# Seven small products for eight in one block product of a sequence DFT, with its sums in accumulating DMAs

## The chip, the core and the metric

The kernel runs on one core of a Trainium2 chip. The metric is the device time of one launch in microseconds, the lower the better; the time of before is the median of three runs. A profile is one execution recorded by the hardware; its times are counted from the first instruction.

Five engines work side by side, each through its own instructions in order: TensorE (PE; PEld is its weight load), VectorE (DVE), ScalarE (ACT), GpSimd (POOL) and SyncE (SP). SP and POOL issue most DMAs, and sixteen DMA engines move the data. On-chip memory has 128 partitions; a tile named 128x1024 has 1024 numbers of four bytes in each. TensorE writes its sums into PSUM, from where ScalarE or VectorE copies them.

## The reference, cut to what matters

```python
def _A_ref(x, dft_seq_re, dft_seq_im, dft_hid_re, dft_hid_im):
    a = jnp.einsum("bsd,ed->bse", x, dft_hid_re)
    b = jnp.einsum("bsd,ed->bse", x, dft_hid_im)
    y = jnp.einsum("ts,bse->bte", dft_seq_re, a) - jnp.einsum("ts,bse->bte", dft_seq_im, b)
    return y
...
xn = _layernorm(x, axis=-1)
s = _A_ref(xn, A_dft_seq_re, A_dft_seq_im, A_dft_hid_re, A_dft_hid_im)
g = _silu(_B_ref(xn, B_w1, B_b1, B_w2, B_b2))
return x + s * g
```

x is 2048 x 512, all in float32. `_B_ref` is a layer norm and an MLP with 1792 hidden units. The change is in the last step: the real part of the DFT along the sequence, a product of a 2048 x 4096 matrix (real and imaginary DFT matrix side by side) with the 4096 x 512 stack of a and b.

## The kernel before

Every product of float32 matrices is made of three matmuls: each factor is split into a rounded part (`hi`, copied by ScalarE into the type float32r) and the rest (`lo`, a subtraction on VectorE), and hi·hi, hi·lo and lo·hi are added in PSUM (`split_into`, L61). A split of a 128x1024 tile is thus one ScalarE and one VectorE instruction, the second waiting for the first, and makes two tiles.

The stages run one after the other: the layer norm and the DFT along the hidden dimension (the results a, b, and sums of their blocks, go to the DRAM tensors `a_d`, `b_d` and `s_d`), the MLP's first layer, its second (`m_units`, seven products of 7 steps each, in the order 1, 4, 2, 5, 6, 3, 7), and the DFT along the sequence.

The DFT along the sequence is a 2 x 2 block product done with seven block products for eight (Strassen-Winograd). The blocks of the left factor are a1, b1, b2 and sums s1 to s4, ready in DRAM; those of the right factor are quarters of the DFT matrices, `ct[m, h, n]` (m: real or imaginary, h: half of the sequence, n: one of 16 rows of 128), and sums of those. Each block product has 16 steps, and a step is 12 matmuls of 128x512 (`multiply_by`, L1009): two halves k of the output's rows, two halves tau of the 1024 columns, three terms. A block product's result fills two PSUM tiles of two banks each; there are four such tiles.

`passes` (L1080) pairs the products: (s4, s3), (a1, s2), (b1, b2), then s1, and b1 again for four steps that `DEFER` (L1081) leaves out of the third pass. A unit (q, n) is step n of pass q. For each unit there are three things to do ahead of its matmuls: `unit_load` (L1099) loads the left blocks (every second unit) and the right one, `unit_sum` (L1116) makes the right sums on VectorE in the held tile `t_hold[n]`, and `unit_split` (L1135) makes the splits. `ahead` (L1152) runs them a fixed number of units before the matmuls, and the loop at L1310 goes through the units; so the order of the instructions on each engine is written out by hand. The same steps for the first units are called in the MLP's last product (L1197 and after, `p == 7`).

Right sums: t = c12 - c22 (for s3), then t - c11 (s2), then c21 + t (b2, in c21's tile), and for s1 c22 is added to t: for even n by an accumulating DMA that POOL issues (L1129, the data in memory are added to the tile), for odd n by a load and a VectorE addition.

Tiles come from pools with a fixed number of places; a new tile waits until the last reader of the place is done. `op` has 39 places of 128x1024 (operands of splits, and `guest` tiles, L51), `lp` seven of the same size in the last stage (`room`, L57), `gp` four (copies of finished products).

The finished blocks are copied out of PSUM by ScalarE (`evacuate`, L1018), joined by VectorE (`after`, L1283), multiplied by the gate silu(z) (`gated`, L1267, which also adds x by an accumulating DMA), and stored (`put_out`, L1271). The last four steps of s1 and the deferred ones of b1 run piece by piece (`piece`, L1332), one quarter of the output after the other, so that the product with the gate, the sum and the store of one quarter (`end`, L1339) lie beside the matmuls of the next.

Of the kernel before, what the change touches and what calls it, by code (L numbers as in the profile page):

```python
# [14 lines left out]
P = 128  # L15
# [5 lines left out]
def fnet_mixer_kernel(ctx: ExitStack, tc: tile.TileContext, x, xT, ct, wt, w1, w2, b1, b2, out):  # L21
# [1058 lines left out]
    passes = [("s4", "s3"), ("a1", "s2"), ("b1", "b2"), ("s1",), ("b1",)]  # L1080
    DEFER = (8, 9, 10, 11)  # L1081
    units = [(q, n) for q in range(4) for n in range(NS)] + [(4, n) for n in DEFER]
    c_raw, c_left, c_ops, t_hold = {}, {}, {}, {}

    def names(q, n):
        return ("b2",) if q == 2 and n in DEFER else passes[q]


    def in_order(q, n):
        return names(q, n)[::-1 if (q, n) in ((1, 0), (2, NS - 1)) else 1]  # L1090

    at = {"load": 0, "sum": 0, "split": 0}

    def c_in(key, src, where):
        t = (guest if where == "op" else room)(f"{key}")
        nc.sync.dma_start(out=t, in_=src)
        return t

    def unit_load(u):  # L1099
        q, n = units[u]  # L1100
        if n % 2 == 0:
            t = room(f"la{q}_{n}")
            for v, name in enumerate(names(q, n)):
                nc.sync.dma_start(out=t[:, v, :].rearrange("p (c e) -> p c e", c=2), in_=left(name, n // 2))
            c_left[q, n // 2] = t
        if q == 0:
            c_raw[u] = {"s4": c_in(f"c22_{n}", ct[1, 1, n], "lp")}
            t_hold[n] = c_in(f"c12_{n}", ct[0, 1, n], "op")
        elif q == 1:
            c_raw[u] = {"a1": c_in(f"c11_{n}", ct[0, 0, n], "lp")}  # L1110
        elif q in (2, 4):
            c_raw[u] = {"b1": c_in(f"c21_{q}_{n}", ct[1, 0, n], "lp" if q == 2 else "op")}
        elif n % 2:
            c_raw[u] = {"s1": c_in(f"d22_{n}", ct[1, 1, n], "lp")}

    def unit_sum(u):  # L1116
        q, n = units[u]
        t = t_hold[n]
        if q < 2:
            raw, = c_raw[u].values()  # L1120
            nc.vector.tensor_sub(t, t, raw)  # L1121
            c_raw[u]["s2" if q else "s3"] = t
        elif q == 2:
            raw = c_raw[u].pop("b1")
            c_ops[u] = {"b1": split_two(raw, f"R2_{n}_b1")} if len(names(q, n)) == 2 else {}
            nc.vector.tensor_add(raw, raw, t)  # L1126
            c_raw[u]["b2"] = raw
            if n % 2 == 0:
                nc.gpsimd.dma_start(out=t, in_=ct[1, 1, n], accum_op=ALU.add)  # L1129
        elif q == 3:  # L1130
            if n % 2:
                nc.vector.tensor_add(t, t, c_raw[u]["s1"])  # L1132
            c_raw[u] = {"s1": t}

    def unit_split(u):  # L1135
        q, n = units[u]
        if n % 2 == 0:
            t = c_left[q, n // 2]
            who = names(q, n)
            if len(who) == 2:  # L1140
                hi, lo = split_two(t, f"L{q}_{n}")
                c_left[q, n // 2] = {name: (hi[:, v, :], lo[:, v, :]) for v, name in enumerate(who)}
            else:
                c_left[q, n // 2] = {who[0]: split(t[:, 0, :], f"L{q}_{n}")}
        ops = c_ops.setdefault(u, {})
        raw = c_raw.pop(u)
        for name in names(q, n):
            if name in raw:
                ops[name] = split_two(raw[name], f"R{q}_{n}_{name}")


    def ahead(what, until):  # L1152
        while at[what] < min(len(units), until):
# [95 lines left out]
    def kept(name):  # L1249
        return gp.tile([P, 2, W], F32, tag="g", name=name)  # L1250
# [150 lines left out]
```

## Time and profile before

| | |
|---|---|
| median of 3 runs | 665.1 us (665.03 to 665.2) |
| the profiled execution | 665.77 us, its span 664.0 us |
| matmuls in the program | 2914, PE busy 658.8 us |
| VectorE, ScalarE, POOL busy | 543.0, 361.5, 50.7 us |
| DMA | 172.81 MB, mean 260 GB/s |
| the sequence DFT's matmuls | 355.34 to 660.23 us |

How to read the rows below: a row of the chain of waits is a start, a length, an engine and a group of instructions that followed each other without a gap. A row of stretches is a time window, each engine's busy time in it with the number of its instructions, the clock granted to TensorE as a share of full speed, the mean busy share of the sixteen DMA engines, and what they moved. The DMA share adds the times that the packets took, so it can pass 1 when packets of several queues overlap. A row of a group is a line of the kernel, an engine and an operation, the tiles written and read, their shapes and a count, then busy time and mean ns of one, and the engine's idle time just before them with what ended it. A row of a tile or line has shortest, median and longest duration in ns and the first and last start.

### The profile page before, as it was taken

The page shows a single profiled execution, that of the slowest core. Times are in us where ns is not written, and L with a number is a line of the kernel's source. Part 1 is how long each engine was busy: PE and PEld are TensorE (multiplying, and loading weights), DVE is VectorE, ACT ScalarE, POOL GpSimd, SP SyncE. Part 2 cuts the span into 40 slices and gives each one's busy share as a digit, 9 for nine tenths or more (in the row PEclk, how much of TensorE's full clock was granted, in tenths as well). Part 3 has the DMA queues.
Part 4 walks back from the last instruction along what each step waited for, and adds up shares of the span by engine and source line. Part 5 has one row for each costly group of instructions (what it writes and reads, how often), then busy time and mean ns, then how long its engine had stood idle before and what let it go on. Part 6 is the DMA issues. An engine that isn't in the chain of part 4 may idle for free.

```text
span 664.0 us, 8219 instructions
## 1 busy us (share of the span) xinstructions
PE 658.8 (99%) x2914; PEld 542.8 (82%) x2914; DVE 543.0 (82%) x584; ACT 361.5 (54%) x420; POOL 50.7 (8%) x84
## 2 busy tenths in 40 slices
PE   9999999999999999999999999999999999999997
PEld 6788888888888888888888888888888888888886
DVE  7899977877777866888979998739877299998986
ACT  6775567545446755555455544456444455646540
POOL 0002000321121100000000000000000001210100
PEclk9999999999999999999999999999999999999999
DMA  9879440987989999798799996416544548996983
GB/s 321 281 254 284 147 155 1 344 313 263 350 297 358 415 412 366 267 392 306 257 396 409 365 330 223 150 57 198 184 154 130 126 134 254 308 257 242 314 255 137
DMA packets 71877, 172.81 MB, mean 260 GB/s; under 512 B 6896, under 2 KB 22812, under 8 KB 71836
## 3 DMA queue, kind: packets, MB, share of 16 engines
q1 hardware_dynamic: 59488, 132.27, 56.7%
q0 software_dynamic: 12032, 39.86, 18.9%
q8 instruction: 23, 0.38, 0.2%
q10 hardware_dynamic: 316, 0.16, 0.1%
q14 instruction: 18, 0.15, 0.1%
HBM read 121.91 MB, written 50.35 MB: 259 GB/s over the span
## 4 chain that ended last, share of the span: by engine, by line
PE 97%; ACT 1%; DVE 1%; DMA 0%; issue 0%; ACTq 0%; DVEq 0%
PE pz L1015 20%; PE px L1015 18%; PE ma L1015 11%; PE hy L830 11%; PE mb L1015 9%; PE hz L830 6%; PE pw L1015 5%; PE q1y L654 3%; PE hx L830 3%; PE pd L418 2%; PE px L1336 2%; PE pw L1336 2%; PE q1z L654 2%; PE pd L406 1%; PE quy L654 1%; PE q1x L654 1%
## 5 line engine op out<-in xcount | busy, mean ns | idle before, releaser
L1121 DVE TENSOR_TENSOR c<-c,c 128x1024 f32<-128x1024 f32 x32 | 38.9, 1216 | 4.1 <-DMA c<-ct 4.1
L81 DVE TENSOR_TENSOR w1l<-w1r,w1h 128x1792 fp32r<-128x1792 f32 x7 | 14.2, 2024 | 20.9 <-ACT w1h L525 20.9
L835 ACT ACTIVATE hc<-hc,b_t 128x1024 f32<-128x1024 f32 (+1 forms) x18 | 17.3, 960 | 24.8 <-DVE hc L875 22.6
L63 DVE TENSOR_TENSOR R_b1l<-c,R_b1h 128x1024 fp32r<-128x1024 f32 x16 | 19.4, 1220 | 13.6 <-ACT R_b1h L62 10.3
L62 ACT ACTIVATE R_s3h<-c 128x1024 fp32r<-128x1024 f32 x16 | 17.0, 1061 | 24.8 <-DVE c L1121 10.8
L1015 PE MATMUL pw<-R_s1h,L 128*128 128x512 f32 x96 | 29.7, 389 | 0.0
L62 ACT ACTIVATE R_b2h<-c 128x1024 fp32r<-128x1024 f32 x16 | 16.9, 1058 | 21.5 <-DVE c L1126 17.0
L63 DVE TENSOR_TENSOR R_s2l<-c,R_s2h 128x1024 fp32r<-128x1024 f32 x16 | 19.5, 1220 | 8.6 <-PE pz L1015 8.6
L62 ACT ACTIVATE R_s2h<-c 128x1024 fp32r<-128x1024 f32 x16 | 17.0, 1061 | 16.8 <-PE px L1015 9.3
L62 ACT ACTIVATE R_s1h<-c 128x1024 fp32r<-128x1024 f32 x16 | 16.4, 1051 | 11.7 <-DVE c L1132 11.7
L63 DVE TENSOR_TENSOR R_s3l<-c,R_s3h 128x1024 fp32r<-128x1024 f32 x16 | 19.5, 1216 | 4.0 <-PE pz L1015 4.0
L62 ACT ACTIVATE R_b1h<-c 128x1024 fp32r<-128x1024 f32 x16 | 16.7, 1053 | 10.7 <-DMA c<-ct 4.7
L1129 POOL DMA_DIRECT2D c<-ct x8 | 7.0, 872 | 201.1 <-DVE c L1126 162.9
L62 ACT ACTIVATE R_a1h<-c 128x1024 fp32r<-128x1024 f32 x16 | 16.9, 1053 | 8.9 <-PE pz L1015 7.2
L1015 PEld LDWEIGHTS pw<-R_s1h,L 128*128 128x128 f32 x96 | 18.0, 188 | 3.8
L63 DVE TENSOR_TENSOR R_b2l<-c,R_b2h 128x1024 fp32r<-128x1024 f32 x16 | 19.4, 1218 | 1.5 <-PE px L1015 1.5
L63 DVE TENSOR_TENSOR R_a1l<-c,R_a1h 128x1024 fp32r<-128x1024 f32 x16 | 19.5, 1218 | 1.3 <-PE px L1015 1.1
L63 DVE TENSOR_TENSOR R_s4l<-c,R_s4h 128x1024 fp32r<-128x1024 f32 x16 | 19.4, 1215 | 0.7 <-PE px L1015 0.7
L1126 DVE TENSOR_TENSOR c<-c,c 128x1024 f32<-128x1024 f32 x16 | 19.6, 1223 | 0.4
L62 ACT ACTIVATE R_s4h<-c 128x1024 fp32r<-128x1024 f32 x16 | 16.8, 1051 | 5.2 <-PE pz L1015 5.0
L62 ACT ACTIVATE w2h<-w 128x1024 fp32r<-128x1024 f32 (+1 forms) x14 | 13.3, 947 | 10.9 <-DVE w L943 3.9
L63 DVE TENSOR_TENSOR R_s1l<-c,R_s1h 128x1024 fp32r<-128x1024 f32 x16 | 18.8, 1218 | 0.1
(1003 smaller groups left out, 2227.3 us busy)
## 6 DMA issues: line engine op xcount, KB each, us to landing
c<-ct SPq DMA_DIRECT2D x68, 512.0 KB, 6.0
m<-h_d SPq DMA_DIRECT2D x48, 512.0 KB, 6.7
h_d<-ht POOLq DMA_DIRECT2D x21, 512.0 KB, 6.4
s_d<-sa SPq DMA_DIRECT2D x32, 256.0 KB, 4.0
la<-s_d SPq DMA_DIRECT2D x32, 256.0 KB, 6.1
h_d<-hc POOLq DMA_DIRECT2D x13, 512.0 KB, 3.9
x<-x SPq DMA_DIRECT2D x16, 256.0 KB, 5.6
sa<-a_d SPq DMA_DIRECT2D x8, 512.0 KB, 6.1
```

The source lines that it names most:

```text
L62: nc.scalar.activation(hi, src, AF.Copy)
L63: nc.vector.tensor_sub(lo, src, hi.bitcast(F32))
L81: nc.vector.tensor_sub(hi_lo[1], src, hi_lo[0].bitcast(F32))
L418: nc.tensor.matmul(dacc[i, m], xt[i, k][px], weights[m * NK + k][pw], start=seen[i, m] == 0, stop=seen[i, m] == 3 * NK - 1)
L654: nc.tensor.matmul(qx[key], a, w, start=p in (1, 5, 2) and n == 0, stop=p in (2, 3, 4) and n == len(terms) - 1, skip_group_check=True)
L830: nc.tensor.matmul(acc[:, tau, :], w[:, W1_AT[p], k * P:(k + 1) * P], r[:, k, :], start=p in (1, 5, 2) and i == 0, stop=p in (2, 3, 4) and ...
L835: nc.scalar.activation(dst, src, AF.Gelu_apprx_tanh, bias=b1_t[:, row:row + 1])
L1015: nc.tensor.matmul(acc[k][:, tau, :], a, c[:, tau, :], start=first and i == 0, stop=last and i == len(terms) - 1, skip_group_check=True)
L1121: nc.vector.tensor_sub(t, t, raw)
L1126: nc.vector.tensor_add(raw, raw, t)
L1129: nc.gpsimd.dma_start(out=t, in_=ct[1, 1, n], accum_op=ALU.add)
L1336: nc.tensor.matmul(acc[KEY[name]][k][:, tau, cols], a[k], c[:, tau, cols], start=False, stop=last and u == us[-1] and i == 2, skip_group_c ...
```

## The change

Seven block products remain, in another order and with other times for the steps ahead of them; one of them, b1, is itself done by seven small products for eight.

1. The order is a1 together with b1's small products, then (s4, s3), then (s2, s1), then b2 alone, whose last four steps go piece by piece at the end. `piece` and `end` now serve b2 alone.
2. b1: its left block (256 rows of output, from `b_d`) and its right one (`ct[1, 0]`) are cut into 2 x 2 parts. Each small product p, in the order 1, 2, 5, 3, 6, 7, 4, has four chunks of six matmuls of 128x512. The right quarters of products 1, 2, 3, 7 are loaded (runs of 2 KB); the sums for 5, 6 and 4 are made in the tiles of product 1 (`H`), each by an accumulating DMA issued after the split of the one before, and the sum for 7 by an accumulating DMA after its load. The left parts lie in one tile `wide` (pool `gp`, now one place of four times the size), loaded in 16 pieces during product 3 of the MLP, and their sums are made there by VectorE.
3. Each of the first three steps of a1 stands alone, then two chunks follow each step, and the last four chunks follow step 15.
4. s1's right sum is no longer finished for even and odd n in two ways: ScalarE copies t (after - c11) into a tile of its own, and an accumulating DMA adds c22. b2's sum is an accumulating DMA of c21 into t, issued after the split for s2.
5. In place of `ahead`, each step ahead has a due place, counted in matmuls before the product that needs it: left loads 96, splits 56, and loads and sums as in the calls below. A list sorted by due place is run as the matmuls are issued; the sort orders the instructions and doesn't hold them to these places.

```diff
-    passes = [("s4", "s3"), ("a1", "s2"), ("b1", "b2"), ("s1",), ("b1",)]
-    DEFER = (8, 9, 10, 11)
+    LEFT, SPLIT = 96, 56
...
+    def unit(names, n, load, total, load_at, total_at=0, after={}):
+        at = place[0]
+        if n % 2 == 0:
+            due(at - LEFT, then(left_in, names, n // 2))
+            due(at - SPLIT, then(left_split, names, n // 2))
+        due(at - load_at, then(load, n))
+        if total:
+            due(at - total_at, then(total, n))
+        for name in names:
+            due(at - SPLIT, then(raw_split, name, n))
+        for name in names:
+            item(12, then(multiply, name, n), [after[name]] if name in after else ())
...
+    def small_load(p, g):
+        if p == 1:
+            small_h[g] = guest(f"H{g}")
+            nc.sync.dma_start(out=small_h[g], in_=quarter(0, 0, g))
+        if p in (2, 3, 7):
+            raw_in((p, g), quarter(*{2: (1, 0), 3: (1, 1), 7: (0, 1)}[p], g), guest if p == 7 else room)
+
+    def small_sum_right(p, g):
+        nc.gpsimd.dma_start(out=raws[p, g], in_=quarter(1, 1, g), accum_op=ALU.add)
+
+    def small_split(p, g):
+        src = raws.pop((p, g)) if p in (2, 3, 7) else small_h[g]
+        small_ops[p, g] = split_two(src, f"S{p}_{g}")
+        if p in (1, 5, 6):
+            nc.gpsimd.dma_start(out=src, in_=quarter(*{1: (0, 1), 5: (1, 1), 6: (1, 0)}[p], g), accum_op=ALU.add)
...
+    def chunk(p, g):
+        at = place[0]
+        due(at - (132 if p == 7 else 108), then(small_load, p, g))
+        if p == 7:
+            due(at - 108, then(small_sum_right, p, g))
+        if g == 0:
+            if p in (5, 3):
+                due(at - SPLIT - 36, then(small_sum, p))
+            due(at - SPLIT - 6, then(small_left_split, p))
+        due(at - SPLIT, then(small_split, p, g))
+        item(6, then(small_mm, p, g), [then(small_after, p)] if g == 3 else ())
+        if g == 3 and p in (2, 6, 7):
+            due(place[0] + (0 if p == 7 else 12), then(small_add, 3 if p == 6 else p))
...
+    a_load = lambda n: raw_in(("a1", n), ct[0, 0, n], guest if n < 4 else room)
...
+    for n in range(NS):
+        unit(("a1",), n, a_load, None, 108, after={"a1": keep_1} if n == NS - 1 else {})
+        ready = 28 if n == NS - 1 else 2 * max(n - 2, 0)
+        for p, g in chunks[given:ready]:
+            chunk(p, g)
+        given = ready
...
+        unit(("s4", "s3"), n, second_load, second_sum, 132, 84,
...
+    def third_sum(n):
+        t = hold[n]
+        nc.vector.tensor_sub(t, t, raws.pop(("c11", n)))
+        raws["s2", n] = t
+        raws["s1", n] = room(f"t{n}")
+        nc.scalar.activation(raws["s1", n], t, AF.Copy)
+        nc.gpsimd.dma_start(out=raws["s1", n], in_=ct[1, 1, n], accum_op=ALU.add)
+
+    def third_late(n):
+        nc.gpsimd.dma_start(out=hold[n], in_=ct[1, 0, n], accum_op=ALU.add)
+        raws["b2", n] = hold[n]
...
+        unit(("s2", "s1"), n, third_load, third_sum, 150, 116,
...
+        due(place[0] - 24 - SPLIT, then(third_late, n))
...
-            gp = early.enter_context(tc.tile_pool(name="gp", bufs=4, reuse_waits="tile"))
+            gp = early.enter_context(tc.tile_pool(name="gp", bufs=1, reuse_waits="tile"))
...
+        if (p, j) == (3, 3):
+            small_left_in()
+        if p == 7 and j > 1:
+            run_tasks(12 * (j - NJ))
```

The joins and the gates keep their form and get new places: o (the finished b1) is joined with a1, gated and stored in the (s4, s3) stage; s4 and s3 are joined with a1 in the (s2, s1) stage; the other joins follow in the b2 stage, where s4, s3 and s1 are gated. All four blocks of two tiles add x by accumulating DMAs; three are stored by POOL, and the fourth, with b2, is finished piece by piece.

322 lines of the change are left out of this document (172 added, 150 removed).

## The prediction

> **What bounds the kernel now.** I read the page's head and its chain of waits first, then the chain in order of time, then stretches of the last stage one by one.
>
> ```profile
> span 664.0 us, 8219 instructions
> PE 658.8 (99%) x2914; PEld 542.8 (82%) x2914; DVE 543.0 (82%) x584; ACT 361.5 (54%) x420; POOL 50.7 (8%) x84
> PE 97%; ACT 1%; DVE 1%; DMA 0%; issue 0%; ACTq 0%; DVEq 0%
> ```
>
> ```profile
> 336.30 19.04 PE ma L1015 x84
> 355.34 2.72 PE px L1015 x12
> ...
> 649.10 11.13 PE px L1336 x66
> ```
>
> The chain (start, length, what, count) is TensorE back to back: 12 matmuls of 128x512 take 2.72 us, so one takes 0.2267 us. The sequence DFT begins at 355.34 and its last matmul ends at 660.23. It is bound by TensorE; fewer matmuls pay, as long as nothing else comes late. How near the others are:
>
> ```profile
> core 0: us, PE busy (x) PEld busy (x) DVE busy (x) ACT busy (x) POOL busy (x), PEclk, DMA share, GB/s
> 341.70:355.30 13.60, 13.60 (x62) 11.26 (x61) 9.80 (x9) 4.18 (x5) 0.00 (x0) 1.00 1.02 403
> 442.40:529.40 87.00, 87.00 (x385) 72.03 (x385) 65.19 (x56) 45.89 (x45) 1.77 (x2) 1.00 0.53 157
> 529.40:605.50 76.10, 76.10 (x338) 63.00 (x337) 70.20 (x63) 41.89 (x44) 10.01 (x10) 1.00 0.85 238
> 341.70:660.20 318.50, 318.50 (x1423) 264.27 (x1421) 265.90 (x249) 161.10 (x166) 17.51 (x20) 1.00 0.71 228
> 509.50:512.50 3.00, 3.00 (x15) 2.46 (x15) 2.62 (x3) 1.07 (x1) 0.00 (x0) 1.00 0.97 172
> 573.40:597.40 24.00, 24.00 (x107) 19.87 (x107) 23.58 (x21) 14.88 (x16) 6.60 (x6) 1.00 1.08 271
> ```
>
> The last two columns decide. DMA share is the packets' time over sixteen engines; 1.08, held for 24 us, is the most this trace shows, and I take it as the ceiling for mixed traffic. Plain loads fill the engines at 403 GB/s (first row), but one accumulating DMA almost alone fills them at 172 (fifth row): 0.524 MB / 172 x 0.97 = 2.96 us of all sixteen engines, where a plain 512 KB load takes 0.524 / 403 x 1.02 = 1.33. The sixth row says the same: 6 accumulates (3.15 MB) in 6.50 MB; the plain 3.36 MB cost 8.5 of 25.9 us, so 2.9 each remain. Divided by the ceilings, an accumulate takes **2.69 us** of the wall and a plain 512 KB **1.30**.
>
> **The change part by part.**
>
> *Matmuls.* Block product b1 was 16 x 12 = 192 matmuls; seven small products of 4 chunks x 6 make 168 of the same 128x512 kind. The other six products keep 192 each: 1344 become 1320. 24 x 0.2267 = **-5.4 us**, all on the chain. The end is the same code (four late pieces, then product, sum and store of quarter tiles), so what lies behind the last matmul stays; I count 0, at most 1 us either way.
>
> *VectorE and ScalarE.*
>
> ```profile
> L1121 DVE TENSOR_TENSOR c<-c,c 128x1024 f32<-128x1024 f32 x29 | 35.3, 1216 | 0.0
> L63 DVE TENSOR_TENSOR R_a1l<-c,R_a1h 128x1024 fp32r<-128x1024 f32 x16 | 19.5, 1218 | 1.3 <-PE px L1015 1.1 <-PE pz L1015 0.2
> L62 ACT ACTIVATE R_a1h<-c 128x1024 fp32r<-128x1024 f32 x16 | 16.9, 1053 | 8.9 <-PE pz L1015 7.2 <-PE px L1015 1.7
> L63 DVE TENSOR_TENSOR L<-la,L 128x512 fp32r<-128x512 f32 x12 | 8.2, 684 | 0.9 <-ACT L L62 0.9
> ```
>
> Right-hand splits go from 112 to 96 + 28 = 124 (+12), right-hand sums on DVE from 56 to 32 (-24, the accumulating DMAs take them over), left splits from 22 wide and 12 narrow to 23 and 16, small sums +4, joins of finished blocks 10 to 12, gate products 6 to 8, and 16 half-tile steps at the end go. 12 x 1.22 - 24 x 1.22 + 1.2 + 2.7 + 4.9 + 2.4 + 2.4 - 10.9 + 2 = about -10 us of DVE, and ScalarE gains 12 x 1.05 + 3.5 + 16 copies x 1.05 = 33 us on 161 in 318. Neither total is a bound. But in the first stretch (a1 with the small products) DVE is dense: until the last right split of small product 7 it has 15 + 24 splits, 8 narrow and 6 wide left splits, 4 sums, 4 joins of the MLP and some 3 splits left of it: 74 us of work, planned over 322 matmuls = 73 us, with 10 more before PE needs it. The sixth row above shows DVE at 23.58 of 24 us with PE never waiting, so alone this costs 0 to 3 us; I take 0, covered by the 56 matmuls (12.7 us) of lead. Small products share PSUM banks; each boundary has 12 matmuls of a1 (2.72 us) over a 128x512 copy or add (0.68 by the last row above): 0, at most 1 us for each of five. Stage boundaries keep the old pattern, two PSUM copies behind 12 matmuls of another product: 0.
>
> *POOL and SP.*
>
> ```profile
> L1129 POOL DMA_DIRECT2D c<-ct x8: 851/870/900, 507.8 to 587.2; - x8
> DMA to landing us min/median/max: 5.4/7.4/10.2
> L1269 POOL DMA_DIRECT2D p<-xT x6: 1195/1204/1307, 573.4 to 626.9; - x6
> DMA to landing us min/median/max: 9.5/10.6/12.5
> ```
>
> Accumulates go from 8 + 6 to 16 small + 32 + 8 gated = 56. Their issue (0.87 to 1.2 us each, some 57 us over 313) is hidden. POOL issues in order: a late DMA of the third stage (c21 into the held tile) waits for a DVE split, and the next s1 sum waits behind it. What waits for the landings is worse: ScalarE's rounding of that operand, behind it on ScalarE and VectorE every later split, and then PE. SP gets 16 strided loads of 2 KB runs in place of 4 KB ones and 16 small pieces for `wide`; both land long before use: 0. The 39 `op` tiles are tight near the end of the third stage (16 held, 12 of splits, 4 of lefts, 2 of s4, 6 of gates make 40), so a gate load may stand on SP until a product frees a tile, and b2's left loads behind it; they have 96 matmuls of lead: 0, at most 3 us.
>
> ```profile
> c<-ct SPq DMA_DIRECT2D x68, 512.0 KB, 6.0
> c<-ct POOLq DMA_DIRECT2D x8, 512.0 KB, 7.4
> p<-xT POOLq DMA_DIRECT2D x6, 512.0 KB, 10.6
> d<-ct SPq DMA_DIRECT2D x8, 512.0 KB, 6.8
> px<-xT SPq DMA_DIRECT2D x2, 512.0 KB, 6.5
> ```
>
> *The DMA engines.* Accumulates +42 x 2.9 = +122 us of packet time; plain transfers change by about nothing (80 loads for the 68 + 8 + 2 of these rows, 48 left halves for 56, `wide` added). Before, the stage holds 0.71 x 318.5 = 226 us; after, 348, and 313 us x 1.08 hold 338. So the average alone is at the ceiling, and the lulls (the row 442.40:529.40 at 0.53) don't return. If the packets of before are inflated by their own crowding, by up to a tenth, it is 325: still 96%. So two stretches in which accumulates lie close decide. I count from the first a1 matmul (place 0) in matmuls of 0.2267 us.
>
> First stretch. Small product 7's last right operand, used at place 318, must land by 298 (a split, 1.05 + 1.22, and the landing, about 2 us). Until then must pass 15 small accumulates (40 us), 16 small and 16 a1 loads (42), eight left halves (5) and four z stores (5): 92 us of wall, in 358 matmuls from place -60: 81 us. Up to eight early loads into guest tiles can land before -60 (-10). Against that, stage 2 asks from place 228 for its own loads, of which four units and two left pairs (13 us) fit the free tiles before the split, and the engines share. 92 - 81 = 11, minus 10, or plus 13: **1 to 24 us late; I take 10**, near the middle of the low half, because the guests surely gain something and the packets of the accumulates keep half the engines.
>
> Third stretch (s2 with s1): per 24 matmuls (5.44 us) two accumulates, one c11 load and a left half: 2 x 2.69 + 1.30 + 0.65 = 7.3 us of DMA. Until the last s1 sum lands, 29 accumulates (78), 16 c11 (21), 16 left halves (10) and six gate loads (8): 117 us, against 26.3 us of lead (116 matmuls) and 79.7 of the stage: 106.
>
> ```profile
> L63 DVE TENSOR_TENSOR R_a1l<-c,R_a1h x16: 1211/1218/1225, 423.9 to 507.5; 128x1024 fp32r<-128x1024 f32 x16
> L1015 PE MATMUL px<-R_a1l,L_0h x8: 389/389/389, 445.2 to 449.9; 128*128 128x512 f32 x8
> ```
>
> Splits ran up to 21 us ahead of PE in the lull of before (423.9 for 445.2), so the work can start 5 to 8 us earlier than planned, and the first c11 loads with it: **0 to 11 us late; I take 4**, as the run ahead takes most of the 11.
>
> Sum: the profiled execution took 665.8 us (664.0 its span): 665.8 - 5.4 + 10 + 4 = 674.4. The runs' median is 0.7 lower: **673.7 us**. Stage by stage, a1 with the small products 81.6 + 10, s4/s3 87, s2/s1 87 + 4, b2 44.
>
> *A rule against a row.* The row 509.50:512.50 gives 172 GB/s for an accumulate. The Trainium skill, DMA: Bandwidth & Descriptors, section "Anatomy of one DMA — SWDGE (gpsimd) path", fits a DMA issued by GpSimd as about 2.0 us and its bytes over 436 GB/s, with no word of accumulating. By it an accumulate's movement would take an estimated 1.2 us, no more than a plain load, and nothing here would be late; the row doesn't agree, with 2.96 us.
>
> **Rivals.**
>
> *Hidden after all (ends faster).* An accumulate's time is mostly its own latency, and engines serve the loads of the other queue meanwhile. At the plain price of 1.33 us the stage needs 226 + 42 x 1.33 = 282 of 313 us, nothing is late, and the time is 665.1 - 5.4 = 659.7; with a wait of 1 to 3 us, up to 663. For it: PE never waited in 573.4 to 597.4 at a share of 1.08. Against: the engines stood at 271 GB/s there; were the latency hidden, the GB/s would stay near 403. It decides if both stretches together are late by less than 5.4 us. It is what the page's rule gives.
>
> *VectorE is the bound of the first stretch.* Its 74 us over 73, and each wait for a landing is lost; the lead takes most, 5 to 8 us come out: 665 to 668. For it: 70.20 of 76.10 us in the third window row. Against: no PE wait there.
>
> *Both stretches at their upper ends:* 665.1 - 5.4 + 24 + 11 = 695, if stage 2's loads really push the accumulates back, and the splits don't run ahead.
>
> **How the numbers follow.** Forecast (late by 7 to 26 us in all, 667 to 686): 0.54. Hidden: 0.27. VectorE: 0.12. Upper ends: 0.07. A measurement can tell 0.2%, 1.3 us, from no change. Faster is the hidden case, 0.27; within 0.2% is over half of the VectorE case, 0.08; slower is the rest, 0.65. The range reaches from the hidden case, 659.5, to 686; the forecast's own is 667 to 686.
>
> **What would show it.** Right: the DMA share near 1.05 from the MLP's last product to the end of small product 7 and again in the s2/s1 stage; ScalarE's rounding of product 7's or s1's operands waiting for DMA; PE gaps there, few in the s4/s3 stage; accumulates landing 15 us and more after issue. Wrong: a PE row without gaps and 24 matmuls less (hidden); PE waiting for VectorE splits whose DMA had long landed (VectorE); an accumulate that moves more than 172 GB/s; gaps at the PSUM boundaries.

## The result, and the profile after

The changed kernel takes 722.28 us (median, 721.24 to 722.62) where the kernel before takes 665.15: a ratio of 1.0855, with a 95% interval of 1.0842 to 1.0868. It is 57 us slower. The forecast had 673.7 us and a range up to 686.0.

The head of the page of the changed kernel answers to the one of before: span, busy time, and the chain that ended last.

```profile
span 720.8 us, 8313 instructions
PE 664.1 (92%) x2890; PEld 541.4 (75%) x2890; DVE 534.5 (74%) x572; ACT 389.1 (54%) x457; POOL 95.7 (13%) x130
PE 5%; DMA 4%; issue 3%; DVE 2%; ACT 1%; SPq 0%; ACTq 0%; DVEq 0%
```

The 24 matmuls are gone (2914 to 2890), yet PE's busy time rose from 658.8 to 664.1 us: some matmuls ran slower. The chain no longer says much, since it breaks off at 608 us; so the next view is what TensorE waited for in the sequence DFT (engine, line and tiles waited for, us in total, times, longest).

```profile
PE small L1217 <- DVE po L1234: 28.6, 1, 28.6
PE pz L1015 <- ACT Rs_11h L62: 6.7, 1, 6.7
PE small L1217 <- ACT po L1229: 5.5, 1, 5.5
PE pz L1015 <- ACT ps L1137: 2.0, 1, 2.0
...
PE pz L1015 <- DVE Rs_8l L63: 0.9, 1, 0.9
```

Before, TensorE ran through this part without a gap. To place the loss, take the first matmul of each stage, from the view of a tile (durations, then first and last start):

```profile
L1015 PE MATMUL py<-Rs_0h,Ls_0h x4: 389/390/390, 477.5 to 479.6; 128*128 128x512 f32 x4
L1015 PE MATMUL pz<-Rs_0h,Ls_0h x4: 389/390/390, 564.6 to 566.6; 128*128 128x512 f32 x4
L1015 PE MATMUL pz<-Rb_0h,Lb x8: 387/394/504, 669.3 to 671.9; 128*128 128x512 f32 x8
```

| stage | matmuls x 0.2267 us | after | late by |
|---|---|---|---|
| a1 with the small products, from 354.7 | 81.6 | 122.8 | 41.2 |
| s4/s3 | 87.0 | 87.1 | 0.1 |
| s2/s1 | 87.0 | 104.7 | 17.7 |
| b2, to 713.98 | 43.9 | 44.7 | 0.8 |
| behind the last matmul | (3.8 before) | 6.8 | 3.0 |

With -5.4 for the matmuls and -0.6 for an earlier start these add up to 56.8 us, the difference of the two spans (720.8 - 664.0). So two stages hold nearly all of it, the two that the prediction named.

Stretches of the first stage, in the columns of the prediction's rows:

```profile
395.00:415.00 20.00, 14.15 (x50) 11.17 (x51) 19.29 (x19) 13.95 (x17) 4.81 (x6) 0.83 1.06 308
415.00:435.00 20.00, 15.91 (x71) 12.85 (x69) 4.81 (x5) 4.86 (x6) 7.51 (x7) 1.00 1.08 300
435.00:455.00 20.00, 0.00 (x0) 0.00 (x0) 6.33 (x7) 5.73 (x8) 0.00 (x0) 0.51 0.97 244
```

The DMA engines are full in all three rows. From 415 to 455 VectorE and ScalarE are nearly empty meanwhile, and in the third row TensorE does nothing. ScalarE's order of time shows what everything waits for (start, length, what, and in brackets the idle time before it with what ended it):

```profile
423.25 1.06 ACT L62 ACTIVATE S_0h<-raw 128x1024 fp32r<-128x1024 f32 x1 [6.63 <-DMA raw<-ct]
432.82 1.06 ACT L62 ACTIVATE S_1h<-raw 128x1024 fp32r<-128x1024 f32 x1 [8.51 <-DMA raw<-ct]
...
442.21 1.06 ACT L62 ACTIVATE S_2h<-raw 128x1024 fp32r<-128x1024 f32 x1 [6.86 <-DMA raw<-ct]
450.67 1.06 ACT L62 ACTIVATE S_3h<-raw 128x1024 fp32r<-128x1024 f32 x1 [7.40 <-DMA raw<-ct]
...
452.58 0.58 ACT L1229 ACTIVATE po<-small 128x512 f32<-128x512 f32 x1
```

These are the four right operands of small product 7. They land some 9 us apart, because POOL issues an accumulate of product 4's sum (into `H`) between each two of product 7's, and SP's loads for s4/s3 run beside them. The last is rounded 96.0 us into the stage; by the forecast's plan it had to land by place 298, that is 67.6 us. TensorE could have begun product 7 with its first operand, split at 425.5. It doesn't, for product 6's bank must be copied out first (last row above), and product 3's sum added (VectorE, L1234). Both stand in their engines' lines behind the splits of product 7's later chunks:

```profile
451.75 1.23 DVE L63 TENSOR_TENSOR S_3l<-raw,S_3h 128x1024 fp32r<-128x1024 f32 x1 [7.23 <-ACT S_3h L62]
...
458.68 0.68 DVE L1234 TENSOR_TENSOR po<-po,small 128x512 f32<-128x512 f32 x1
```

So all of product 7, two steps of a1 and product 4 (72 matmuls) are still to do at 459.5. And the first of them are slow:

```profile
459.51 0.77 PE L1217 MATMUL small<-S_0h,SLh 128*128 128x512 f32 x1 [28.59 <-DVE po L1234]
460.07 0.63 PE L1217 MATMUL small<-S_0l,SLh 128*128 128x512 f32 x1
460.50 0.63 PE L1217 MATMUL small<-S_0h,SLl 128*128 128x512 f32 x1
```

They start 0.43 us apart in place of 0.227. The shorter wait before it, of 5.5 us up to 406.4, is of the same kind: ScalarE's copy of an earlier product (L1229, at 405.76) stood behind two roundings that waited for their loads.

In the third stage, the longest gap begins with a load that came late. First SyncE's rows, then VectorE's:

```profile
624.18 0.33 SPq L1103 DMA_DIRECT2D rawc<-ct  x1
```

```profile
622.94 1.22 DVE L63 TENSOR_TENSOR Rs_10l<-t,Rs_10h 128x1024 fp32r<-128x1024 f32 x1
631.93 1.23 DVE L1282 TENSOR_TENSOR raws<-raws,rawc 128x1024 f32<-128x1024 f32 x1 [7.78 <-DMA rawc<-ct]
```

SP stood for a place in `lp` until the split at 622.94 had read t; the load then took 7.7 us at a DMA share of 1.05, and the subtraction, ScalarE's copy of t and the rounding `Rs_11h` followed in turn. The waits of 0.8 to 0.9 us for `Rs_6l`, `Rs_8l`, `Rs_10l` have another cause, found below.

### The profile page after: what moved, and what is told of

It reads as the page before. It is cut to its first block, busy times and chain, and to the rows that moved or that the text cites. A ratio compares the mean times of both kernels' runs of the same rounds, so it can differ in the third digit from the quotient of the medians.

```text
span 720.8 us, 8313 instructions
## 1 busy us (share of the span) xinstructions
PE 664.1 (92%) x2890; PEld 541.4 (75%) x2890; DVE 534.5 (74%) x572; ACT 389.1 (54%) x457; POOL 95.7 (13%) x130
## 5 line engine op out<-in xcount | busy, mean ns | idle before, releaser
L1285 ACT ACTIVATE t<-raws 128x1024 f32<-128x1024 f32 x16 | 17.0, 1060 | 54.5 <-DVE raws L1282 27.3
L1217 PE MATMUL small<-S_0h,SLh 128*128 128x512 f32 x14 | 6.7, 480 | 34.1 <-DVE po L1234 28.6
L1282 DVE TENSOR_TENSOR raws<-raws,rawc 128x1024 f32<-128x1024 f32 x16 | 19.5, 1220 | 7.8 <-DMA rawc<-ct 7.8
L1286 POOL DMA_DIRECT2D t<-ct x16 | 13.8, 860 | 80.7 <-ACT t L1285 80.7
L1204 POOL DMA_DIRECT2D H<-ct x12 | 18.7, 1670 | 41.4 <-DVE S_0l L63 34.9
L1269 DVE TENSOR_TENSOR raws<-raws,raws 128x1024 f32<-128x1024 f32 x16 | 19.5, 1221 | 0.0
L1289 POOL DMA_DIRECT2D raws<-ct x16 | 13.7, 859 | 39.2 <-DVE Rs_14l L63 6.6
L830 PE MATMUL hy<-yt_1l,w1h 128*128 128x512 f32 x42 | 16.4, 389 | 0.0
L830 PE MATMUL hy<-yt_0h,w1h 128*128 128x512 f32 x42 | 16.4, 389 | 0.0
L830 PE MATMUL hy<-yt_0h,w1l 128*128 128x512 f32 x42 | 16.4, 389 | 0.0
L830 PE MATMUL hy<-yt_1h,w1h 128*128 128x512 f32 x42 | 16.4, 389 | 0.0
L830 PE MATMUL hy<-yt_0l,w1h 128*128 128x512 f32 x42 | 16.4, 389 | 0.0
L830 PE MATMUL hy<-yt_1h,w1l 128*128 128x512 f32 x42 | 16.3, 389 | 0.0
## 6 DMA issues: line engine op xcount, KB each, us to landing
rawa<-ct SPq DMA_DIRECT2D x16, 512.0 KB, 10.5
```

What stands on the lines that cost most here:

```text
L830: nc.tensor.matmul(acc[:, tau, :], w[:, W1_AT[p], k * P:(k + 1) * P], r[:, k, :], start=p in (1, 5, 2) and i == 0, stop=p in (2, 3, 4) and ...
L1204: nc.gpsimd.dma_start(out=src, in_=quarter(*{1: (0, 1), 5: (1, 1), 6: (1, 0)}[p], g), accum_op=ALU.add)
L1269: nc.vector.tensor_sub(hold[n], hold[n], raws["s4", n])
L1282: nc.vector.tensor_sub(t, t, raws.pop(("c11", n)))
L1285: nc.scalar.activation(raws["s1", n], t, AF.Copy)
L1286: nc.gpsimd.dma_start(out=raws["s1", n], in_=ct[1, 1, n], accum_op=ALU.add)
```

## The experiments

Each time is that of one execution, with the kernel before beside it at 664.9 to 665.7 us; the changed kernel's own runs spread over 1.4 us, and no smaller difference of whole times is read here. Stage times are differences of first matmuls as above, good to 0.1 us; s4/s3 took 87.0 or 87.1 us in every run.

### Accumulates made plain

The first run makes the 16 accumulates of the small sums and the 32 of the third stage plain loads into the same tiles, so that the second summand takes the first one's place; the other two do it for the 16 or the 32 alone.

```diff
-        nc.gpsimd.dma_start(out=raws[p, g], in_=quarter(1, 1, g), accum_op=ALU.add)
+        nc.gpsimd.dma_start(out=raws[p, g], in_=quarter(1, 1, g))
```

(and so at L1204, L1286, L1289)

> The 48 accumulating DMAs of the sums (16 in the small products, 32 in the s2/s1 stage) become plain DMAs of the same bytes from the same queue at the same places, so the right sums are left out and the old content is overwritten; matmuls, splits, waits and queue order stay. Theory A (the accumulates' time on the DMA engines, 2.9 us against 1.33 us, is what comes late): the pauses of TensorE vanish in both stretches, 660 to 666 us. Rival B (the order on POOL and the short lead of the loads, whatever the DMAs do): 712 us or more. Rival C (VectorE's density in the first stage): the first stage keeps 30 us of its delay, about 695 us.

> Only the 16 accumulates of the small products become plain DMAs (their sums are left out). Theory A: the first stage, 122.8 us after the change, goes back to 82 to 88 us and the s2/s1 stage keeps its 17.6 us of delay: 681 to 688 us. Rivals B and C: the first stage stays at 115 us or more, 712 us or more.

> Only the 32 accumulates of the s2/s1 stage become plain DMAs (c22 into t, c21 into the held tile; the sums are left out). Theory A: the s2/s1 stage goes from 104.7 to 87 us, the first stage keeps its delay: 700 to 706 us. Rival B: 715 us or more.

| | whole | first stage | third stage |
|---|---|---|---|
| after | 722.28 | 122.8 | 104.7 |
| all plain | 684.58 | 100.3 | 92.7 |
| the 16 small ones plain | 702.65 | 99.6 | 111.2 |
| the 32 of the third stage plain | 706.97 | 122.7 | 92.7 |

The accumulates' extra time is worth 22.5 us of the first stage (23.2 alone) and 12.0 of the third. The first number is the prediction's: 16 x (2.69 - 1.30) = 22.2. The second is no price, since something else holds that stage at 92.7, as the last runs show. The windows of the run with all plain show it too:

```profile
395.00:415.00 20.00, 15.91 (x60) 12.62 (x59) 19.06 (x19) 12.63 (x15) 5.77 (x8) 0.83 0.99 366
415.00:435.00 20.00, 11.54 (x51) 9.21 (x50) 11.37 (x11) 11.89 (x14) 0.00 (x0) 0.90 1.03 399
```

In the second row the same full engines move 399 GB/s in place of 300. But 18.7 and 5.7 us of lateness stay.

### b1 as one product again

The small products are undone: b1 runs whole beside a1, 192 matmuls, in the new order of products.

```diff
-        unit(("a1",), n, a_load, None, 108, after={"a1": keep_1} if n == NS - 1 else {})
...
+        unit(("a1", "b1"), n, ab_load, None, 108, after={"a1": keep_1, "b1": copy_o} if n == NS - 1 else {})
```

> The small products are undone: b1 is one block product of 192 matmuls beside a1 again, with its right block loaded plainly, and the order and the other stages of the changed kernel stay. All theories: the first stage takes its 384 matmuls, 87 us, without pauses. Theory A and B: the s2/s1 stage keeps 12 to 18 us of delay, 682 to 688 us. If the new order and the 32 accumulates cost nothing by themselves (the third stage was late only as an echo of the first): 665 to 668 us.

It took 688.33 us: the first stage 87.0 for 384 matmuls of 87.0, with no wait; the third 107.4. So the third stage's lateness is its own and no echo of the first, and the whole loss of the first belongs to the small products.

### Reordering, with the accumulates kept

Four ways to help product 7, and one for the third stage:

```diff
-            due(place[0] + (0 if p == 7 else 12), then(small_add, 3 if p == 6 else p))
+            due(place[0] + {7: 0, 2: 12, 6: 60}[p], then(small_add, 3 if p == 6 else p))
```

> VectorE's addition of small product 3's result (due 12 matmuls after product 6, ahead of product 7) is moved behind product 7 (due 60 after product 6). Theory A1 (only the late landing of product 7's operands counts): the first stage stays at 120 to 123 us, 720 us. Theory B1 (product 7's first chunk has its operands at 425.5 us and PE is free at 431, but waits for this addition, which VectorE has in line behind the splits of later chunks that wait for DMA): chunks 0 to 2 run while the rest lands, and the first stage takes 108 to 115 us, 708 to 715 us.

The wait moved to ScalarE's copy at L1229, which stands behind the same splits; first stage 123.5, whole 723.82.

```diff
-            raw_in((p, g), quarter(*{2: (1, 0), 3: (1, 1), 7: (0, 1)}[p], g), guest if p == 7 else room)
+            raw_in((p, g), quarter(*{2: (1, 0), 3: (1, 1), 7: (0, 1)}[p], g), room if (p, g) in ((2, 0), (2, 1)) else guest)
```

> The raw right quarters of small products 2 (chunks 2, 3) and 3 go into tiles of the large pool op instead of the 7 places of lp, for which SP stood 11 us (355.4 to 366.4) with all later loads behind it. Theory A1: the DMA engines were full in that time (share 1.04), so nothing is gained: first stage 119 to 123 us, 718 us or more. Theory B2 (the queue that stands costs the time): product 7's loads come some 10 us earlier, first stage 108 to 114 us, 707 to 714 us.

First stage 122.2, whole 722.82: earlier places gain nothing where the engines are full.

```diff
     def second_load(n):
-        raw_in(("s4", n), ct[1, 1, n])
-        raw_in(("s3", n), ct[0, 1, n], guest)
+        queue = nc.gpsimd if n < 4 else nc.sync
+        raw_in(("s4", n), ct[1, 1, n], None, queue)
+        raw_in(("s3", n), ct[0, 1, n], guest, queue)
```

> The right loads of the first four units of the s4/s3 stage (8 x 512 KB) are issued on POOL, behind the accumulates of small products 6 and 7, and not on SP beside them. Theory A1 (the engines share, and these 10.6 us of loads delay the accumulates): product 7's last operand lands 8 to 11 us earlier, first stage 111 to 115 us, 711 to 715 us. If the accumulates go at their own pace whatever runs beside: first stage 120 us or more.

With the next stage's first loads behind the accumulates, product 7's last operand was rounded at 439.86 in place of 450.67, 10.8 us earlier; the stage took 114.3 (8.5 less), the third 108.8, the whole 717.35.

```diff
-        due(at - SPLIT, then(small_split, p, g))
+        due(at - (SPLIT if p == 1 else 30), then(small_split, p, g))
```

> The right splits of small products 2 to 7 are due 30 matmuls ahead instead of 56, so that the PSUM copy by ScalarE that frees a bank for the next small product stands in its line ahead of that product's later splits; the addition of product 3 stays behind product 7. Theory B (PE waits for a bank because its copy is in line behind splits that wait for DMA): the first stage falls from 122.8 us to 108 to 114 us, 708 to 714 us. Theory A1 (only the landing of the last operand counts): 119 us or more.

With this and L1234 late, the long wait shrank to 12.2 us, but others of 4.9, 4.8 and 3.0 came up; first stage 119.7, whole 719.74. The order of the lines decides where TensorE stands, hardly for how long.

```diff
-                     (2, 6, then(gate_load, 0, 1)), (2, 9, then(gate_open, 0, 1)),
+                     (3, 0, then(gate_load, 0, 1)), (3, 0, then(gate_load, 1, 0)), (3, 1, then(gate_load, 1, 1)),
...
```

> The six gate tiles of the s2/s1 stage are loaded and opened in the b2 stage instead. Theory A (accumulates alone delay the third stage): 104.7 us of third stage fall by 3 to 5 us, the 7.8 us of gate loads being gone from the DMA engines, but the waits of PE for the splits of every second unit from unit 6 on stay. Theory B3 (the gate tiles take places of op, so that the splits from unit 6 on come late): those waits of 0.8 to 0.95 us vanish, third stage 92 to 99 us, 710 to 716 us.

The six gate tiles out of the third stage: it takes 96.5 us (8.2 less), the whole 710.28. The prediction had 8 us for their transfers in its sum of 117, and 0 to 3 more for the places that they take. The waits of 0.8 to 1.0 us for every second unit are still there, so it is not the gates' places that cause them.

> e9 together with the first four units of s4/s3 issued behind the accumulates and the gates in the b2 stage; all 48 accumulates stay. If the effects add (order 10, sharing 5, gates 12): 693 to 700 us, with the DMA share at 1.0 and above in both crowded stages. If they are the same time counted twice: 703 us or more.

> e9 with the gates in the b2 stage, and all 48 accumulates as plain DMAs (their sums are left out). Theory A with B (accumulates and the order they block are all of the loss): first stage 82 to 88 us, third 87 to 92 us, 660 to 670 us. If plain bytes alone already fill the DMA engines in the first stage: first stage 93 us or more, 673 us or more.

The edits together (late loads, splits 30 ahead, late gates) took 710.99 us with a first stage of 122.5: no better than late gates alone. The third stage's 96.8 is theirs. The splits at 30 and late gates with all 48 accumulates plain took 685.41 (first 100.9, third 93.0), the same as plain without them. So neither rest is a matter of these orders.

### The small sums on GpSimd

Each quarter is loaded once, and POOL adds them in place of the accumulates (with splits at 30 and late gates):

```diff
+        t = quarters[(*dst, g)]
+        nc.gpsimd.tensor_add(t, t, quarters[(*other, g)])
```

> The 16 right sums of the small products are made by GpSimd additions in memory from quarters that are loaded once each (16 plain loads in place of 16 loads and 16 accumulates); the order of e9 and the late gates stay, and so do the 32 accumulates of the third stage. Theory A: the first stage's DMA falls from about 100 us to about 55 us, its pauses vanish, 82 to 88 us for it, and 680 to 688 us in all. If GpSimd's additions take VectorE's time on the shared memory ports: VectorE's splits get longer than 1.22 us and the first stage takes 95 us or more.

It took 711.90 us, the first stage 123.1, although the DMA share fell to 0.23 between 395 and 415. The rows are VectorE's, in order of time, and then GpSimd's line with its durations in ns (shortest, median, longest):

```profile
413.75 3.40 DVE L63 TENSOR_TENSOR S_0l<-Q,S_0h 128x1024 fp32r<-128x1024 f32 x1
417.07 3.41 DVE L63 TENSOR_TENSOR S_1l<-Q,S_1h 128x1024 fp32r<-128x1024 f32 x1
...
428.19 1.21 DVE L63 TENSOR_TENSOR S_3l<-Q,S_3h 128x1024 fp32r<-128x1024 f32 x1
```

```profile
L1201 POOL TENSOR_TENSOR Q<-Q,Q x16: 2342/3347/13007, 375.6 to 450.0; 128x1024 f32<-128x1024 f32 x16
```

The same subtraction takes 3.4 us while GpSimd adds, and 1.21 when it doesn't. VectorE becomes the bound. The Trainium skill, SBUF — State Buffer, section "SBUF: two separate sides", has a pair of ports that VectorE's operations with two inputs and GpSimd share as an exclusive lock; by that one of them stands while the other works, and these rows agree.

### What is left without the accumulates' time

The 16 second summands of the small sums are not transferred at all, which leaves b1 with 16 half-megabyte transfers, as many as b1 whole has, in place of 32:

```diff
     def small_sum_right(p, g):
-        nc.gpsimd.dma_start(out=raws[p, g], in_=quarter(1, 1, g), accum_op=ALU.add)
+        pass
...
-        if p in (1, 5, 6):
-            nc.gpsimd.dma_start(out=src, in_=quarter(*{1: (0, 1), 5: (1, 1), 6: (1, 0)}[p], g), accum_op=ALU.add)
```

> The sixteen DMAs that bring the second summand of the seven products' right sums are left out, so the sums are wrong by that summand and the transfers are those of twelve chunks and fewer; everything else stays as in the changed kernel. Theory bytes (what is left of the first stage's excess once the accumulates are made plain is the plain bytes of the sixteen transfers): the first stage takes 82 to 90 us in place of 122.8, the DMA share between 400 and 450 us falls below 0.9, and the whole is 681 to 690 us. Theory order (what is left is the line of copies, additions and splits, or the places of the operands): the first stage stays at 97 us or more and the whole at 696 us or more.

687.29 us, first stage 89.2. With the 16 plain and the rest unchanged it was 99.6, so 10.4 of the 18.0 us left there were the plain bytes of these transfers. TensorE has one wait left in the stage, and the window before it shows which engine is full:

```profile
PE small L1215 <- DVE po L1232: 4.3, 1, 4.3
```

```profile
395.00:415.00 20.00, 20.00 (x89) 16.31 (x88) 20.00 (x20) 16.28 (x19) 0.00 (x0) 1.00 0.97 362
```

VectorE is at 20.00 of 20 us, and in its order of time in the next run it works from 384 to 427 without a pause. That one wait, for the addition of product 3's sum, is followed by matmuls at half pace. In the next run, whose first stage is 88.5 - 81.6 = 6.9 us late, the wait and the half pace make 6.8: VectorE's lag, and no DMA time. Part of the lag is the order again: just ahead of the addition (423.65 in the next run) VectorE does three splits for product 4 and a sum for the stage after, from 419.11 on, which TensorE doesn't need yet. To put the addition ahead of them here was not tried.

The next run leaves out also the 16 late transfers of the third stage (L1289, b2's second summand) and has late gates:

> As the run before it, with the sixteen late transfers of the third stage (second summands of its right sides) left out too, and the six gate tiles loaded and opened in the stage after it. Theory bytes: the third stage falls from 104.7 to 87 or 88 us, so that the gain of the 24 matmuls shows, and the whole is 660 to 668 us. Theory order: the third stage stays at 92 to 93 us as in the run with all transfers plain, and the whole is not under 667 us, about 673 us if the first stage falls and the third does not.

673.80 us, first stage 88.5, third 92.7: not the 87 or 88 of theory bytes. With 16 transfers and the gate loads less it is the 92.7 of the run with all plain; so this floor is an order. Its rows on ScalarE and VectorE show a ring (order of time, one engine each):

```profile
571.82 1.06 ACT L1283 ACTIVATE t<-raws 128x1024 f32<-128x1024 f32 x1 [2.61 <-DVE raws L1280]
572.79 1.04 ACT L62 ACTIVATE Ls_4h<-lefts 128x1024 fp32r<-128x1024 f32 x1
573.73 1.04 ACT L62 ACTIVATE Rs_8h<-raws 128x1024 fp32r<-128x1024 f32 x1
...
584.14 1.06 ACT L1283 ACTIVATE t<-raws 128x1024 f32<-128x1024 f32 x1 [2.61 <-DVE raws L1280]
```

```profile
570.57 1.22 DVE L1280 TENSOR_TENSOR raws<-raws,rawc 128x1024 f32<-128x1024 f32 x1
573.86 1.23 DVE L63 TENSOR_TENSOR Ls_4l<-lefts,Ls_4h 128x1024 fp32r<-128x1024 f32 x1 [2.07 <-ACT Ls_4h L62]
...
577.27 1.22 DVE L1280 TENSOR_TENSOR raws<-raws,rawc 128x1024 f32<-128x1024 f32 x1
```

The subtraction ends, ScalarE's copy of t starts; the copy and a rounding end, VectorE's splits start; the splits end, the next subtraction starts. Each engine idles 2 to 3 us in every turn, and two units take 584.14 - 571.82 = 12.32 us where TensorE needs 48 x 0.2267 = 10.88. When the lead is used up, TensorE pays the 1.44 us once in two units: the waits for `Rs_6l`, `Rs_8l`, `Rs_10l`, with a slower restart. To break the ring, the copy is put behind the roundings of the unit before:

```diff
     def third_sum(n):
...
+    def third_copy(n):
+        t = hold[n]
         raws["s1", n] = room(f"t{n}")
         nc.scalar.activation(raws["s1", n], t, AF.Copy)
...
+        due(place[0] - 24 - 103, then(third_copy, n))
```

> As the run without small sums and late transfers, with one edit: ScalarE's copy of t stands 13 places later, behind the roundings of the unit before it. Theory ring: the 5.7 us that the third stage keeps over 87 come from a closed ring of three steps, VectorE's subtraction, then ScalarE's copy ahead of two or three roundings, then VectorE's splits that need those roundings, then the next subtraction: 12.33 us for two units where TensorE needs 10.88. With the copy behind, the third stage takes 87 to 88 us, the waits for Rs_6l, Rs_8l, Rs_10l and Rs_12l go, and the whole is 667 to 669 us. Theory places (the operands' tiles come free too late): 92 to 93 us as before, 673 to 674 us.

669.06 us, the third stage 87.1 without a wait, as theory ring had it: the view of what TensorE waited for has one row from 340 us on.

```profile
PE small L1215 <- DVE po L1232: 4.4, 1, 4.4
```

Then the same edit with all transfers in place:

> The changed kernel with the gate tiles late and the copy of t 13 places later, all transfers and sums in place. If the ring adds to the accumulates' time, the third stage falls from 96.4 us to 91 to 93 and the whole from 710 to 705 to 707 us. If the DMA engines alone bound the third stage, it stays at 95 to 97 us and the whole at 709 to 711 us, or rises by up to 3 us, since the accumulates into t are issued 2.9 us later.

716.53 us, 2.5 above the upper end of what was expected, the third stage 98.6: the time is not gone with the ring. With the accumulates in it the stage stands on two bounds that lie close, and here the DMA engines are the later one: ScalarE waits up to 3.9 us for a landing, and the share is 1.06 in this stretch of it:

```profile
600.00:620.00 20.00, 19.19 (x83) 15.07 (x82) 10.57 (x9) 9.69 (x10) 4.82 (x6) 1.00 1.06 260
```

The whole is 6.2 us above late gates alone (710.28), of which the third stage has 2.1, the first 1.1 and b2 with the end 2.4. The trace shows where most of it comes from. At the end of the third stage TensorE loses 3.5 us that late gates alone doesn't lose: b2's product takes the PSUM tile of s2, and ScalarE's copy of s2 stands in line behind the roundings of b2's first operands (the wait is that for `ps`, L1137). Less this pause the stage is 95.1 us, 1.3 under late gates alone. Then b2's first matmuls run at half pace for a while, which is 1.9 of the 2.4.

> b1 as one product of 192 matmuls as before the change, the other products in the new order, the gate tiles late and the copy of t 13 places later. First stage 87 us as in the run with b1 whole. Theory ring plus gates: third stage 91 to 97 us in place of 107.4, whole 672 to 679 us. If neither adds here: 105 to 108 us and 686 to 689 us. In no case under the time before the change.

680.58 us, first stage 87.1, third 98.8. It lies between the two forecasts, and the third stage lost 8.6 of 107.4, about what late gates alone gained. None of the versions reaches the time before. A larger pool `lp`, which would test the places directly, doesn't fit into the memory and stays open.

## Why the prediction was wrong, point by point

**What bounds the kernel, and the mechanism: right.** The two stretches named are the ones that are late, with a DMA share of 1.05 to 1.08, ScalarE waiting for product 7's operands, and no gap in s4/s3. Of the signs, landings of 15 us and more came for product 7 (10.5 to 32.1 us) and not for the sums of the third stretch (5.4 to 13.0). The direction was right; the size was off by a factor of four: 59 us late where the forecast had 14.

**Matmuls, -5.4 us: right.** 2890, the busy row says.

**The price of an accumulate, 2.69 us of wall against 1.30: right.** 22.2 us for sixteen, 22.5 measured. By the fit that the Trainium skill gives (DMA: Bandwidth & Descriptors, section "Anatomy of one DMA — SWDGE (gpsimd) path") a load that accumulates would cost what a plain one does; the runs disagree, by these 22.5 us.

**"1 to 24 us late; I take 10": the step that failed.** The stage was 41.2 us late, in two parts. Product 7's last operand was rounded 28.4 us behind the plan (96.0 for 67.6), beyond the upper end of 24. And behind it came 26.8 us of stage (450.67 to 477.5) where the plan had 14.0, another 12.8. The first part is a demand taken too low. From place -60, at 341.1, to that rounding the DMA engines were full without a lull (columns as above):

```profile
341.10:450.60 109.50, 83.00 (x349) 66.63 (x347) 70.59 (x66) 51.49 (x58) 22.96 (x22) 0.90 1.06 319
```

That is 109.5 us, where the terms 92 and 13 make 105. So of the two corrections the guests that "surely gain something" (-10) gained nothing: the first of the stage's right operands landed at 343.3, behind place -60, and more guests, when tried, gained nothing either (122.2 for 122.8). The loads of the next stage (+13) came in full: putting the first eight of them behind, 10.4 us by the plain price, made that operand 10.8 us earlier. So it was no help that the accumulates' packets "keep half the engines", the other reason for a low value, which no row shows. Setting the forecast near the middle of the low half was wrong, since the terms were no error bars but transfers that all had to pass. The second part was priced in another sentence.

**"each boundary has 12 matmuls of a1 ... 0, at most 1 us for each of five": failed, and it hid the 12.8.** Gaps at the PSUM boundaries were among the signs of being wrong. The boundary was costed as one copy or addition under 12 matmuls. It should have been costed at its place in the line: behind four splits that wait for DMA. Product 7's wait thus began with its first chunk and not with its last, TensorE had 72 matmuls to do when all had landed, and it did the first at half pace. Moving the two instructions alone helped by 3 us at most, as the splits then stand late. So the 12.8 is the price of a late landing in this order of work, and none of the edits cut it off by itself. "Stage boundaries keep the old pattern ...: 0" failed in the same way at the last border: s2's copy (at 668.23) stood on ScalarE behind two roundings, the first of which waited for a load of b2's left block, and the opening of a gate. TensorE lost 2.2 us there, and 3 to 5 in some of the other runs.

**VectorE "I take 0": wrong by 7 us, and the rival had it.** "each wait for a landing is lost; the lead takes most, 5 to 8 us come out" was the VectorE rival, and with the transfers gone the first stage is 7.6 us late (89.2) with VectorE at 20.00 of 20. The mechanism was not quite the rival's: in the next run VectorE lost no wait for a landing from 384 to 427, it had too much to do, and the addition that TensorE needed stood late in its line. In the changed kernel it is covered by the DMA's lateness (VectorE waits there for the landings). The same runs bear on the hidden rival: with the small sums' transfers left out, the late ones too, and the ring broken, the kernel still takes 669.06 us, 3.4 more than the one before beside it. In this order the seven products don't pay even where those sums are free.

**"0 to 11 us late; I take 4" in the third stretch: too low, since the run ahead didn't come.** It took 17.7. The sum itself came near: from the first accumulate's issue (537.65) to the landing of the last s1 sum (655.9) went 118.3 us, where the sum had 117. That is partly luck, since the mean share over it was 1.00 and not the ceiling. But the work was to start "5 to 8 us earlier than planned", and the first accumulate was issued 26.9 us ahead of the stage where the plan had 26.3. So the 11 stayed whole; why the start was not earlier was not tried. The gate loads' 8 us, which were in the sum, are about the 8.2 by which the stage got shorter without them. Two things were not in it: the wait for s2's copy, above, and the ring that the new copy of t closed with the subtraction and the splits, 12.32 us for 10.88. Its turns stand in the changed kernel too (the copies of t at 593.97, 606.29 and 618.62), and the waits for `Rs_6l`, `Rs_8l` and `Rs_10l` with the slower restart come to 3.9 us. It is worth 5.6 us on its own (92.7 to 87.1). The prediction counted the copies as 16 x 1.05 us of ScalarE, an engine with time to spare, and did not ask what stood before and behind them. The parts don't add: 12.0 us go when the transfers are plain, 8.2 when the gates are late, and to break the ring helps fully only when the DMA engines don't hold the stage.

**The end, "0, at most 1 us either way": wrong by 3.** The last stores of finished blocks now come late, since their accumulates of x landed late (POOL, in order of time):

```profile
709.02 0.54 POOL L1417 DMA_DIRECT2D out<-ps  x1 [7.02 <-DMA ps<-xT]
711.80 0.53 POOL L1417 DMA_DIRECT2D out<-ps  x1 [2.24 <-DMA ps<-xT]
```

They are issued in the last 12 of the span's 720.8 us; that this sets the end was read, not tried.

**Slow matmuls after a pause: no price in the prediction.** They took 5.7 us of the first stage's 41.2 (2.7 behind the pause of 5.5, 1.8 behind that of 28.6, 1.2 about shorter ones) and 2.6 behind the third stage's pause of 6.7, counted from the starts of the matmuls beyond 0.2267 us each.

## What to carry to other kernels

Replacing arithmetic by transfers pays only in a stretch whose DMA engines have room for the added bytes *and* for what the next stage asks for at the same time; sum all of it against the stretch's own time, and take the sum as it stands. A wait for a landing costs more than its own lateness where a PSUM copy that TensorE needs stands in line behind it, and because TensorE restarts slowly. A copy put on an idle engine isn't free when it stands between two steps of another: write down the ring of who waits for whom and compare one turn of it with TensorE's time for the same units.

## What the runs showed of the hardware

TensorE's matmuls of 128x512 start 0.43 us apart after a pause of 4 us or longer, for 3.5 to 5.3 us in the changed kernel (at 406.4, 459.5 and 635.3) and 3 to 6 us in all runs; the first microsecond or so after the pause can still be at full pace. After the changed kernel's pauses of 2.0 us and of under 1 us only the first one or two start later. Between 2 and 4 us both occur: behind 3.3 us before b2 in the last run they are slow, behind 3.4 us at 428.3 in the run with GpSimd's sums they are not. The granted clock in the window 435 to 455, all pause, is 0.51, and 0.50 from 459.5 to 461.5, where the matmuls start 0.43 us apart. The Trainium skill, TensorE: Matmul & The Clock Gate, section "Part 1: The HAM clock gate (the "warmup" mystery)", says that about 3.4 us without work halve the clock and about 3.4 us of work restore it; these rows agree in the doubled spacing, and the slow stretch lasted up to 5.3 us here.

GpSimd's addition of 128x1024 float32 took 2.34 us at best and 3.35 in the median beside VectorE, and made VectorE's subtraction 3.4 us long in place of 1.22. An accumulating DMA of 512 KB cost 1.4 us more of a full stretch than a plain one (22.5 us for sixteen).
